# A transformer block in split fp32: the moving operand of every split matmul is read from its two halves in turn

## The chip, the cores and the metric

The kernel runs on one core of a Trainium2 chip. The metric is the device time of one execution in microseconds: the median of the runs of the kernel as it was is 2450.31 us. The engines are named as the profile names them: PE is TensorE (PEld its weight loads), DVE is VectorE, ACT is ScalarE, POOL is GpSimd, SP is the engine that issues most DMAs.

## The reference

One block over 2048 tokens of width 512, all in fp32. The first half is linear attention with 32 heads of 16 and a learned feature map; the second a mixture of 8 experts in which every token uses all 8 (K = E = 8), so nothing is sparse.

```python
h  = x + A(layernorm(x))
h2 = h + B(layernorm(h))

# A: x[S=2048, D=512], H=32 heads, Dh=16
q, k, v = split(x @ wqkv)
phi(q) = concat(softmax(q @ w_phi), softmax(-(q @ w_phi)))      # per head
o = phi_q (phi_k^T v) / (phi_q . sum(phi_k) + 1e-6)
A = o @ wo
# B: E=8 experts, F=1792
cw = softmax(x @ wg), normalized over all 8
B  = sum_e cw[:, e] * (gelu(x @ w1[e]) @ w2[e])
```

## The kernel before, in words

**Split products.** Each fp32 operand of the large products is split by `split` (lines 58 to 61) into a high part, which ScalarE rounds to the fp32r format, and a low part, the rest, which VectorE subtracts. A product of two split operands is three fp32r matmuls, `mm3` (lines 63 to 68): low times high, high times low, high times high, all added up in one PSUM tile. The first operand of `mm3` is stationary (128 columns of weights), the second is moving: 512 columns of a [128, 512] tile, read from the first to the last. Every matmul loads its own weights. All large products go through `mm3`: the projections (`project`), the experts' first layer (`product`), and the second layer (`product2`, `finish`).

**Stages.** The 2048 tokens are 16 tiles of 128 rows (`NT`), four tiles make a chunk of 512 (`TC`). In the attention stage `steps` walks over the tiles; a table `STAGES` gives each piece of work a lag, so that in one turn several tiles are in different pieces. There the tile of tokens, transposed, is stationary, and a projection weight [128, 512] is moving, so the 512 output columns are the 512 features. `fold` (line 119) multiplies the key and query weights by the feature maps beforehand: it transposes a weight on TensorE, and multiplies it by a block-diagonal [128, 128] matrix `bd`, which GpSimd builds at the start from `w_phi` with selects (lines 920 to 927). `wsplit` (line 101) splits the value and output weights as they are. `q_out` adds the attention's result to x and stores the tile of h in DRAM (`hbuf`); each tile of h is later read once, by `load_h` or in `finish`.

**Experts.** `q_ntrans` transposes the normalized h, so that 512 tokens of a chunk are the columns of a moving operand. The experts' products are arranged in blocks of 2 x 2 with seven products in place of eight (names `m1` to `m7`); their block sums are made on VectorE and split again. In the first layer (`quad`, `product`, into the PSUM tiles `ps`) the expert weights are stationary and 512 tokens move; ScalarE takes the gelu of the result, and VectorE multiplies it by the token's gate, which lies in the token's column of `CW` (loaded from `cwT`, one row of 512 gates per expert and chunk, made by `gate_rows`). In the second layer (`down`, `product2`, into `pacc`) that hidden block is the moving operand. Results are added up in DRAM by DMA (`macc`), and at the end `result` and `finish` load them, transpose them back to token rows, add h and store the output, 128 rows at a time.

**What sets the order.** The order on each engine is the order in which the code issues, with the lags of `STAGES` and the generators `moe`, `quad`, `fetch` and `result` interleaved. SP's queue issues loads of x, weights and h and stores of h and the output; POOL's queue issues the additions to `macc`. Tiles of SBUF come from two pools, `s4` (43 buffers) and `s2` (14), PSUM from `ps` and `pacc`, four banks each.

Of the kernel before, what the change touches and what calls it, by code (L numbers as in the profile page):

```python
# [8 lines left out]
F32 = mybir.dt.float32  # L9
F32R = mybir.dt.float32r  # L10
AF = mybir.ActivationFunctionType
ALU = mybir.AluOpType
AX = mybir.AxisListType

P = 128
# [6 lines left out]
def block_kernel(ctx: ExitStack, tc: tile.TileContext, x, wqkv, w_phi, wo, wg, w1, w2, out):  # L22
# [35 lines left out]
    def split(hi, lo, src, eng=nc.vector):  # L58

        nc.scalar.activation(hi, src, AF.Copy)  # L60
        return eng.tensor_tensor(lo, src, hi.bitcast(F32), op=ALU.subtract)  # L61

    def mm3(out_, a, b, first, last):

        (ah, al), (bh, bl) = a, b
        nc.tensor.matmul(out_, al, bh, start=first, stop=False, skip_group_check=True)  # L66
        nc.tensor.matmul(out_, ah, bl, start=False, stop=False, skip_group_check=True)  # L67
        nc.tensor.matmul(out_, ah, bh, start=False, stop=last, skip_group_check=True)  # L68
# [13 lines left out]


    st, low = {}, {}
    hbuf = [dram.tile([P, D], F32, name=f"h{t}") for t in range(NT)]
    cwT = dram.tile([E, S], F32, name="cwT")

    def load_x(lo, hi):
        for t in range(lo, hi):
            st["a", t] = s2()  # L90
            nc.sync.dma_start(st["a", t], x[t * P:(t + 1) * P, :])

    def load_w(w):

# [5 lines left out]

    def wsplit(src, eng=nc.vector):
        w = s4([P, 2, D], F32R)
        split(w[:, 0], w[:, 1], src, eng)
        return w[:, 0], w[:, 1]

    def split_all(raws, eng=nc.vector):
# [17 lines left out]
    def fold(raws, w, bd):  # L124

        wT = [s2() for _ in range(KD)]
        for b in range(KD):
            p = ps()
            for k in range(KD):
                nc.tensor.transpose(p[:, k * P:(k + 1) * P], raws[k // 2][:, k % 2, b * P:(b + 1) * P], ident)  # L130
            nc.scalar.activation(wT[b], p, AF.Copy)
            yield
        for k in range(KD):
            p = ps()
            for b in range(KD):
                nc.tensor.matmul(p[:, b * P:(b + 1) * P], wT[b][:, k * P:(k + 1) * P],  # L136
                                 bd[:, b].rearrange("p j f -> p (j f)"), start=True, stop=True)
            t = s4([P, 2, D], F32R)
            low["w"] = split(t[:, 0], t[:, 1], p)
            w.append((t[:, 0], t[:, 1]))  # L140
            yield

# [148 lines left out]

    def q_otrans(t):
        st["r", t] = s2()
        nc.sync.dma_start(st["r", t], x[t * P:(t + 1) * P, :])
        p = transposed(st.pop(("o", t)), ps_acc())
        o = st["O", t] = s4([P, 2, KD, P], F32R)
        split(o[:, 0], o[:, 1], p)

    def q_out(t):
        p = project(st.pop(("O", t)), wos, ps_acc())  # L300
        r = st["h", t] = st.pop(("r", t))
        nc.vector.tensor_tensor(r, p, r, op=ALU.add)
        nc.sync.dma_start(hbuf[t], r)
        norm_stats(r, t)


# [42 lines left out]
    def gate_rows(t, lag):  # L349

        c, j = divmod(t, TC)
        if j < TC - 1 or (c >= 2) != (lag > 29):
            return
        p = ps_acc()
        for j in range(TC):
            nc.tensor.transpose(p[:E, j * P:(j + 1) * P], cw[:, c * TC + j, :], ident)
        row = work.tile([E, 512], F32, name="row")
        nc.scalar.activation(row, p[:E], AF.Copy)
        nc.sync.dma_start(cwT[:, c * 512:(c + 1) * 512], row)

    X = {}
# [288 lines left out]

    def load_h(t, slot=s2):
        r = slot([P, D])
        nc.sync.dma_start(r, hbuf[t])
        return r

    def put_out(t, blocks, r):
# [36 lines left out]
    def finish(h, gs):  # L693

        old = {}

        def seeds(dst, src):
            for a, b in zip(dst, src):
                seed(a, b)

        def ready(m):
            for g in gs:
                if (g, m) not in G:
                    operand2(g, m)

        def add(g, m, p, first=False):
            for _ in product2(g, m, p, first):
                pass

        def run_(m, p):  # L710
            for g in gs:
                add(g, m, p)

        def block(i, c, p, r):
            for d in range(2):
                nc.vector.tensor_tensor(r[:, d], p[d], r[:, d], op=ALU.add)
            old[i, c] = r


        pa = [ps_acc(), ps_acc()]  # L720
        add(gs[0], "m1", pa, True)
        yield
        pd = [ps_acc(), ps_acc()]
        add(gs[0], "m5", pd, True)
        yield
        hs = [load_h(h * HALF + i, s4) for i in range(TC, HALF)]
        h0 = [s4([P, 2, D]) for _ in range(TC // 2)]
        for i, r in enumerate(h0):
            for j in range(2):
                nc.sync.dma_start(r[:, j, :], hbuf[h * HALF + 2 * i + j])  # L730
        pb, pc = [ps(), ps()], [ps(), ps()]
        for m in ("m5", "m6"):
            diffs(gs[1], m)
        operand2(gs[1], "m5")
        add(gs[1], "m1", pa)
        seeds(pb, pa)
        r11 = load_block(h, 0, 0)
        yield
        ready("m6")
        add(gs[1], "m5", pd)  # L740
        s5 = s4([P, 2, 512])
        for d in range(2):
            nc.scalar.activation(s5[:, d], pd[d], AF.Copy)
        for c in range(2):
            nc.gpsimd.dma_start(macc[h, BLOCK[c, 1]], s5, accum_op=ALU.add)
        yield
        ready("m2")
        run_("m6", pb)
        seeds(pc, pb)
        r22 = load_block(h, 1, 1)  # L750
        yield
        ready("m7")
        r12 = load_block(h, 0, 1)
        run_("m2", pa)
        block(0, 0, pa, r11)
        yield
        ready("m3")
        ready("m4")
        run_("m7", pc)
        block(1, 1, pc, r22)  # L760
        yield
        run_("m3", pb)
        r21 = load_block(h, 1, 0)
        block(0, 1, pb, r12)
        yield
        ops = [G.pop((g, "m4")) for g in gs]

        def last(d):
            sl = slice(d * P, (d + 1) * P)
            for (wh, wl), (xh, xl) in ops:  # L770
                for i in range(2):
                    mm3(pc[d], (wh[:, i, sl], wl[:, i, sl]), (xh[:, i], xl[:, i]), False, True)

        def sum_(d, i):

            sl = slice(i * 2 * P, (i + 1) * 2 * P)
            nc.vector.tensor_tensor(r21[:, d, sl], pc[d][:, sl], r21[:, d, sl], op=ALU.add)

        def back(d, p, i):

            src = (r11, r21)[d // 2][:, d % 2]
            for j in (2 * i, 2 * i + 1):
                nc.tensor.transpose(p[:, j * P:(j + 1) * P], src[:, j * P:(j + 1) * P], ident)
            o = h0[i][:, :, d * P:(d + 1) * P]
            nc.vector.tensor_tensor(o, p[:, i * 2 * P:(i + 1) * 2 * P].rearrange("p (j f) -> p j f", j=2), o, op=ALU.add)

        def store(lo, hi, i, eng=nc.sync):
            a = (h * HALF + 2 * i) * P
            eng.dma_start(out[a:a + 2 * P, lo * P:hi * P].rearrange("(j p) f -> p j f", p=P),
                              h0[i][:, :, lo * P:hi * P])  # L790

        def turn(d, p):
            if d >= 2:
                for i in range(2):
                    sum_(d - 2, i)
            for i in range(2):
                back(d, p[i], i)

        last(0)
        for d in range(2):  # L800
            turn(d, [ps_acc()] * 2)
        for t in range(TC, HALF):
            n = put_out(h * HALF + t, [r12, r22], hs[t - TC])
            put_store(h * HALF + t, hs[t - TC])
            if t == TC + 1:
                with tc.issue_after(n.ins):
                    turn(2, [ps_acc()] * 2)
                for i in range(2):
                    store(0, 3, i)
        with tc.issue_after(n.ins):  # L810
            last(1)
        turn(3, [ps_acc() for _ in range(2)])
        store(3, 4, 0, nc.scalar)
        store(3, 4, 1)
        yield
# [101 lines left out]
    norm_stats(st["a", 0], 0)  # L917


    bd = s2([P, H // HB, HB, Dh])  # L920
    for b in range(H // HB):
        nc.gpsimd.affine_select(out=bd[:, b], in_=phi_raw[:, b:b + 1, :].to_broadcast([P, HB, Dh]),
                                pattern=[[-Dh, HB], [0, Dh]], base=0, channel_multiplier=1,
                                compare_op=ALU.is_ge, fill=0.0)
        nc.gpsimd.affine_select(out=bd[:, b], in_=bd[:, b],
                                pattern=[[Dh, HB], [0, Dh]], base=Dh - 1, channel_multiplier=-1,
                                compare_op=ALU.is_ge, fill=0.0)

    x_norm(0)
# [37 lines left out]
```

## Time and profile before

| | us |
|---|---|
| median of 3 runs | 2450.31 (2450.18 to 2450.43) |
| span of the profiled execution | 2449.4 |
| PE busy | 2442.2 (100%) |
| PEld busy | 2037.8 (83%) |
| DVE busy | 2161.9 (88%) |
| ACT busy | 1759.9 (72%) |
| POOL busy | 500.4 (20%) |
| mean granted TensorE clock | 1.000 |

Busy time of PE counts overlapping matmuls once; the mean of a group of matmuls (389 to 391 ns for 512 columns) contains the part that overlaps its neighbours, and ends are modelled. The distance between starts says what one matmul costs in a row of them. The attention stage ends at about 340 us, the rest is the experts.

### The profile page before, as it was taken

To read this page: it belongs to the slowest core of one execution; us is meant where nothing else is said; L and a number is where in the kernel's file an instruction comes from. 1 tells how busy PE (TensorE), PEld (TensorE's weight loads), DVE (VectorE), ACT (ScalarE), POOL (GpSimd) and SP (SyncE) were. 2 spreads that over 40 slices of the span, in tenths; PEclk is the share of its full clock that TensorE was granted. 3 is DMA by queue.
4 is the path that set the end of the run, shared out by engine and by line. 5 is a ranking of instruction groups with operands and counts; after the bars stand their busy time and mean duration, and the time that the engine had idled before them with its cause. 6 is when DMAs were issued, how large, how long until landed. Compare 5 with 4: busy or idle time off the path is not lost.

```text
span 2449.4 us, 32135 instructions
## 1 busy us (share of the span) xinstructions
PE 2442.2 (100%) x11340; PEld 2037.8 (83%) x11340; DVE 2161.9 (88%) x3205; ACT 1759.9 (72%) x2891; POOL 500.4 (20%) x568
## 2 busy tenths in 40 slices
PE   9999999999999999999999999999999999999999
PEld 8888888888888888888888888888888888888887
DVE  7677999988989989889898998999889889898998
ACT  4343578777777777777777777777777777777774
POOL 4475101111111111111111331111111111111121
PEclk9999999999999999999999999999999999999999
DMA  3002347787777887877879898987877777877877
GB/s 113 26 14 70 109 173 164 146 168 158 147 158 151 164 165 140 169 151 151 166 143 206 180 203 159 227 174 153 161 157 150 159 163 148 168 143 163 160 154 183
DMA packets 174386, 370.80 MB, mean 151 GB/s; under 512 B 15216, under 2 KB 80240, under 8 KB 174224
## 3 DMA queue, kind: packets, MB, share of 16 engines
q0 software_dynamic: 62560, 206.60, 51.2%
q1 hardware_dynamic: 110336, 161.97, 20.6%
q8 instruction: 89, 1.46, 0.2%
q14 instruction: 73, 0.60, 0.1%
q10 hardware_dynamic: 1328, 0.18, 0.0%
HBM read 157.34 MB, written 218.69 MB: 154 GB/s over the span
## 4 chain that ended last, share of the span: by engine, by line
PE 98%; DVE 1%; ACT 0%; POOL 0%; issue 0%; ACTq 0%; POOLq 0%
PE pacc L66 16%; PE pacc L68 16%; PE pacc L67 16%; PE ps L66 15%; PE ps L68 15%; PE ps L67 15%; PE pacc L230 1%; PE ps L283 1%; PE pacc L161 1%; PE pacc L261 1%; PE pacc L332 0%; PE ps L136 0%; DVE s L61 0%; ACT s L60 0%; PE ps L113 0%; PE ps L161 0%
## 5 line engine op out<-in xcount | busy, mean ns | idle before, releaser
L61 DVE TENSOR_TENSOR s<-s,s 128x1024 fp32r<-128x1024 f32 (+1 forms) x806 | 762.8, 960 | 155.0 <-ACT s L60 146.2
L60 ACT ACTIVATE s<-s 128x512 fp32r<-128x512 f32 (+1 forms) x806 | 673.8, 842 | 11.6 <-DVE s L514 5.9
L66 PE MATMUL pacc<-s,s 128*128 128x512 f32 x1728 | 674.9, 391 | 0.8 <-ACT s L262 0.8
L67 PE MATMUL pacc<-s,s 128*128 128x512 f32 x1728 | 672.5, 389 | 0.3 <-DVE s L61 0.3
L68 PE MATMUL pacc<-s,s 128*128 128x512 f32 x1728 | 672.7, 389 | 0.0
L66 PE MATMUL ps<-s,s 128*128 128x512 f32 x1664 | 649.8, 391 | 0.2 <-ACT ps L569 0.2
L67 PE MATMUL ps<-s,s 128*128 128x512 f32 x1664 | 648.0, 389 | 0.0
L68 PE MATMUL ps<-s,s 128*128 128x512 f32 x1664 | 647.9, 389 | 0.0
L553 ACT ACTIVATE s<-pacc 128x512 f32<-128x512 f32 x756 | 447.0, 595 | 188.8 <-PE pacc L68 183.6
L564 ACT ACTIVATE ps<-ps 128x512 f32<-128x512 f32 x448 | 262.1, 586 | 175.3 <-DVE ps L616 106.0
L68 PEld LDWEIGHTS pacc<-s,s 128*128 128x128 f32 x1728 | 324.4, 188 | 67.9
L66 PEld LDWEIGHTS pacc<-s,s 128*128 128x128 f32 x1728 | 324.4, 188 | 67.5 <-ACT s L262 0.9
L67 PEld LDWEIGHTS pacc<-s,s 128*128 128x128 f32 x1728 | 324.4, 188 | 67.2 <-DVE s L61 0.8
L68 PEld LDWEIGHTS ps<-s,s 128*128 128x128 f32 x1664 | 312.3, 188 | 65.0
L66 PEld LDWEIGHTS ps<-s,s 128*128 128x128 f32 x1664 | 312.3, 188 | 64.5 <-ACT ps L569 0.5
L67 PEld LDWEIGHTS ps<-s,s 128*128 128x128 f32 x1664 | 312.5, 188 | 64.2 <-DVE s L61 0.3
L555 POOL DMA_DIRECT2D acc0m<-s x189 | 162.1, 858 | 856.9 <-ACT s L553 835.4
L565 DVE TENSOR_TENSOR s<-ps,s 128x512 f32<-128x512 f32 x448 | 302.9, 685 | 34.9 <-ACT ps L564 31.3
L555 POOL DMA_DIRECT2D acc1m<-s x175 | 149.5, 854 | 799.2 <-ACT s L553 782.6
L514 DVE TENSOR_TENSOR s<-s,s 128x1024 f32<-128x1024 f32 x224 | 272.9, 1219 | 0.1
L569 ACT ACTIVATE ps<-ps 128x512 f32<-128x512 f32 x226 | 132.0, 584 | 74.0 <-PE ps L68 73.8
L486 DVE TENSOR_TENSOR s<-s,s 128x1024 fp32r<-128x1024 f32 x111 | 135.0, 1216 | 0.0
(110 smaller groups left out, 1799.5 us busy)
## 6 DMA issues: line engine op xcount, KB each, us to landing
acc0m<-s POOLq DMA_DIRECT2D x196, 512.0 KB, 5.6
acc1m<-s POOLq DMA_DIRECT2D x184, 512.0 KB, 5.5
s<-in_B_w_dram SPq DMA_DIRECT2D x224, 256.0 KB, 5.7
s<-in_B_w_dram SPq DMA_DIRECT2D x111, 512.0 KB, 5.2
s<-in_A_x_dram SPq DMA_DIRECT2D x32, 256.0 KB, 2.8
s<-cwT SPq DMA_DIRECT2D x16, 512.0 KB, 5.0
h<-s SPq DMA_DIRECT2D x16, 256.0 KB, 2.0
s<-h SPq DMA_DIRECT2D x16, 256.0 KB, 7.0
```

Source lines behind the costliest of these rows:

```text
L60: nc.scalar.activation(hi, src, AF.Copy)
L61: return eng.tensor_tensor(lo, src, hi.bitcast(F32), op=ALU.subtract)
L66: nc.tensor.matmul(out_, al, bh, start=first, stop=False, skip_group_check=True)
L67: nc.tensor.matmul(out_, ah, bl, start=False, stop=False, skip_group_check=True)
L68: nc.tensor.matmul(out_, ah, bh, start=False, stop=last, skip_group_check=True)
L486: nc.vector.tensor_tensor(sl, s, sh.bitcast(F32), op=ALU.subtract)
L514: nc.vector.tensor_tensor(r, B[a], B[b], op=ALU.subtract)
L553: nc.scalar.activation(e[:, d], p[d], AF.Copy)
L555: return nc.gpsimd.dma_start(macc[h, m], e, accum_op=ALU.add)
L564: nc.scalar.activation(src, src, AF.Gelu_apprx_tanh)
L565: nc.vector.tensor_tensor(B[b][:, q % 2], src, CW[h, e][:, int(b[2]) - 1], op=ALU.mult)
L569: nc.scalar.activation(dst, src, AF.Copy)
```

## The change

`mm3` no longer reads the 512 columns of its moving operand from first to last. It reads columns 0, 256, 1, 257, 2, 258 and so on: one from the first half, one from the second. The output is written without steps, so output column 2a + b is made from moving column 256b + a. Three matmuls, their weights and their sizes are as before.

So that each product still comes out right, the data is laid out anew:

- **Projections.** Output columns are features. The moving weights now hold the even columns first and the odd columns second, so that reading the halves in turn gives the features in order. `wsplit` writes them so (its source is read with a step of two), and `fold` does so by a `bd` with even and odd features apart (eight selects 64 wide and four 128 wide, in place of four and four) and a stepped read of its PSUM tile.
- **Tokens.** Each of the experts' two layers moves the 512 tokens once, and turns their order once. A tile therefore holds every fourth row of its chunk of 512: tile r of chunk c has rows 512c + 4i + r. After two turns the tokens stand in natural order. The loads of x (`x_rows`) and the stores of h (`rows`) step over rows, 2 KB each as before; the loads of h take 128 rows in a row. h is now one DRAM tile per chunk.
- **Gates.** Between the two layers the tokens have been turned once, so `gate_rows` turns the gates' row once with a stepped read.

```diff
+    def halves(v):
+        return v.rearrange("p (b a) -> p a b", b=2)
+
     def mm3(out_, a, b, first, last):
-        (ah, al), (bh, bl) = a, b
+        (ah, al), (bh, bl) = a, (halves(v) for v in b)
+        out_ = out_.rearrange("p (a b) -> p a b", b=2)
         nc.tensor.matmul(out_, al, bh, start=first, stop=False, skip_group_check=True)
         nc.tensor.matmul(out_, ah, bl, start=False, stop=False, skip_group_check=True)
         nc.tensor.matmul(out_, ah, bh, start=False, stop=last, skip_group_check=True)
...
-    hbuf = [dram.tile([P, D], F32, name=f"h{t}") for t in range(NT)]
+    hbuf = [dram.tile([TC * P, D], F32, name=f"h{c}") for c in range(NT // TC)]
...
+    def rows(v, r):
+        return v.rearrange("(i r) d -> r i d", r=TC)[r]
+
+    def x_rows(t):
+        c, r = divmod(t, TC)
+        return rows(x[c * TC * P:(c + 1) * TC * P, :], r)
+
+    def h_rows(t):
+        c, j = divmod(t, TC)
+        return hbuf[c][j * P:(j + 1) * P, :]
...
     def wsplit(src, eng=nc.vector):
         w = s4([P, 2, D], F32R)
-        split(w[:, 0], w[:, 1], src, eng)
+        hi, lo = (w[:, i].rearrange("p (b a) -> p b a", b=2) for i in range(2))
+        split(hi, lo, src.rearrange("p (a b) -> p b a", b=2), eng)
         return w[:, 0], w[:, 1]
...
-                                 bd[:, b].rearrange("p j f -> p (j f)"), start=True, stop=True)
+                                 bd[:, b].rearrange("p l j f -> p (l j f)"), start=True, stop=True)
             t = s4([P, 2, D], F32R)
-            low["w"] = split(t[:, 0], t[:, 1], p)
+            hi, lo = (t[:, i].rearrange("p (l b w) -> p l b w", l=2, b=KD) for i in range(2))
+            low["w"] = split(hi, lo, p.rearrange("p (b l w) -> p l b w", l=2, b=KD))
...
-        nc.sync.dma_start(hbuf[t], r)
+        nc.sync.dma_start(rows(hbuf[t // TC], t % TC), r)
...
-        nc.scalar.activation(row, p[:E], AF.Copy)
+        nc.scalar.activation(row.rearrange("e (a b) -> e a b", b=2), halves(p[:E]), AF.Copy)
...
-    bd = s2([P, H // HB, HB, Dh])
+    bd = s2([P, H // HB, 2, HB, Dh // 2])
     for b in range(H // HB):
-        nc.gpsimd.affine_select(out=bd[:, b], in_=phi_raw[:, b:b + 1, :].to_broadcast([P, HB, Dh]),
-                                pattern=[[-Dh, HB], [0, Dh]], base=0, channel_multiplier=1,
-                                compare_op=ALU.is_ge, fill=0.0)
+        for l in range(2):
+            src = phi_raw[:, b:b + 1, :].rearrange("p o (f l) -> p o f l", l=2)[:, :, :, l]
+            nc.gpsimd.affine_select(out=bd[:, b, l], in_=src.to_broadcast([P, HB, Dh // 2]),
+                                    pattern=[[-Dh, HB], [0, Dh // 2]], base=0, channel_multiplier=1,
+                                    compare_op=ALU.is_ge, fill=0.0)
```

The order of the instructions on each engine is as before, but for two things. The first is on GpSimd at the start, where `bd` is built (`s_165` before, `s_153` after). Before:

```order
L152 TENSOR_TENSOR rs<-rs,mhalf 128x1
L80 AFFINE_SELECT hmask<-hmask 128x4
L922 AFFINE_SELECT s_165<-phi_raw 128x128 x2
L925 AFFINE_SELECT s_165<-s_165 128x128 x2
L922 AFFINE_SELECT s_165<-phi_raw 128x128 x2
L925 AFFINE_SELECT s_165<-s_165 128x128 x2
L152 TENSOR_TENSOR rs<-rs,mhalf 128x1 x2
```

After:

```order
L171 TENSOR_TENSOR rs<-rs,mhalf 128x1
L85 AFFINE_SELECT hmask<-hmask 128x4
L943 AFFINE_SELECT s_153<-phi_raw 128x64 x4
L946 AFFINE_SELECT s_153<-s_153 128x128 x2
L943 AFFINE_SELECT s_153<-phi_raw 128x64 x4
L946 AFFINE_SELECT s_153<-s_153 128x128 x2
L171 TENSOR_TENSOR rs<-rs,mhalf 128x1 x2
```

Four selects have become eight of half the width; the rest keeps its place. The second is on TensorE in the experts' part, where a first-layer product into `ps` is followed by a second-layer product into `pacc` (with what each instruction waits for; `PE_49` is TensorE's own count of finished work). Before:

```order
L66 MATMUL ps<-s_2861,s_9202 128x512 [waits Activation_49]
L67 MATMUL ps<-s_2862,s_9201 128x512
L68 MATMUL ps<-s_2861,s_9201 128x512
L66 MATMUL ps<-s_2861,s_9202 128x512
L67 MATMUL ps<-s_2862,s_9201 128x512
L68 MATMUL ps<-s_2861,s_9201 128x512
L66 MATMUL pacc<-s_9295,s_9292 128x512
L67 MATMUL pacc<-s_9296,s_9291 128x512 [waits DVE_49]
```

After:

```order
L71 MATMUL ps<-s_2853,s_9194 128x512 [waits Activation_49]
L72 MATMUL ps<-s_2854,s_9193 128x512
L73 MATMUL ps<-s_2853,s_9193 128x512
L71 MATMUL ps<-s_2853,s_9194 128x512
L72 MATMUL ps<-s_2854,s_9193 128x512
L73 MATMUL ps<-s_2853,s_9193 128x512
L71 MATMUL pacc<-s_9287,s_9284 128x512 [waits PE_49]
L72 MATMUL pacc<-s_9288,s_9283 128x512 [waits DVE_49]
```

The matmuls stand where they stood; the first into `pacc` now also waits for an earlier matmul of TensorE itself. The built program has 858 such waits, before it had 48.

More of the change, by code (lines that the diff above doesn't have):

```diff
@@ L90, in load_x @@
             st["a", t] = s2()
-            nc.sync.dma_start(st["a", t], x[t * P:(t + 1) * P, :])
+            nc.sync.dma_start(st["a", t], x_rows(t))
     def load_w(w):
@@ L293, in q_otrans @@
         st["r", t] = s2()
-        nc.sync.dma_start(st["r", t], x[t * P:(t + 1) * P, :])
+        nc.sync.dma_start(st["r", t], x_rows(t))
         p = transposed(st.pop(("o", t)), ps_acc())
@@ L652, in load_h @@
         r = slot([P, D])
-        nc.sync.dma_start(r, hbuf[t])
+        nc.sync.dma_start(r, h_rows(t))
         return r
@@ L729, in finish @@
             for j in range(2):
-                nc.sync.dma_start(r[:, j, :], hbuf[h * HALF + 2 * i + j])
+                nc.sync.dma_start(r[:, j, :], h_rows(h * HALF + 2 * i + j))
         pb, pc = [ps(), ps()], [ps(), ps()]
@@ L917, in block_kernel @@
     norm_stats(st["a", 0], 0)
-    bd = s2([P, H // HB, HB, Dh])
+    bd = s2([P, H // HB, 2, HB, Dh // 2])
     for b in range(H // HB):
-        nc.gpsimd.affine_select(out=bd[:, b], in_=phi_raw[:, b:b + 1, :].to_broadcast([P, HB, Dh]),
-                                pattern=[[-Dh, HB], [0, Dh]], base=0, channel_multiplier=1,
-                                compare_op=ALU.is_ge, fill=0.0)
+        for l in range(2):
[3 more added lines that the diff above has]
+                                    compare_op=ALU.is_ge, fill=0.0)
         nc.gpsimd.affine_select(out=bd[:, b], in_=bd[:, b],
-                                pattern=[[Dh, HB], [0, Dh]], base=Dh - 1, channel_multiplier=-1,
+                                pattern=[[0, 2], [Dh, HB], [0, Dh // 2]], base=Dh - 1, channel_multiplier=-1,
                                 compare_op=ALU.is_ge, fill=0.0)
```

## The prediction

> **What bounds the kernel now.** I read the page's totals first, then its chain of waits, then the groups of instructions, and last the windows and the timeline of TensorE alone.
>
> ```profile
> span 2449.4 us, 32135 instructions
> PE 2442.2 (100%) x11340; PEld 2037.8 (83%) x11340; DVE 2161.9 (88%) x3205; ACT 1759.9 (72%) x2891; POOL 500.4 (20%) x568
> PE 98%; DVE 1%; ACT 0%; POOL 0%; issue 0%; ACTq 0%; POOLq 0%
> L66 PE MATMUL pacc<-s,s 128*128 128x512 f32 x1728 | 674.9, 391 | 0.8 <-ACT s L262 0.8
> L67 PE MATMUL pacc<-s,s 128*128 128x512 f32 x1728 | 672.5, 389 | 0.3 <-DVE s L61 0.3
> L68 PE MATMUL pacc<-s,s 128*128 128x512 f32 x1728 | 672.7, 389 | 0.0
> L66 PE MATMUL ps<-s,s 128*128 128x512 f32 x1664 | 649.8, 391 | 0.2 <-ACT ps L569 0.2
> L67 PE MATMUL ps<-s,s 128*128 128x512 f32 x1664 | 648.0, 389 | 0.0
> L68 PE MATMUL ps<-s,s 128*128 128x512 f32 x1664 | 647.9, 389 | 0.0
> L66 PEld LDWEIGHTS ps<-s,s 128*128 128x128 f32 x1664 | 312.3, 188 | 64.5 <-ACT ps L569 0.5
> ```
>
> TensorE is never free: the chain that ended last is 98% its own, and the idle time ahead of its groups is under 1 us each. The three lines of a split product run 3 x (1728 + 1664) = 10,176 times with 512 columns each. Their 389 to 391 ns are not what one costs, since matmuls overlap; that is read from starts:
>
> ```profile
> 1200.09 0.39 PE L66 MATMUL ps<-s,s 128*128 128x512 f32 x1
> 1200.32 0.39 PE L67 MATMUL ps<-s,s 128*128 128x512 f32 x1
> ...
> 1211.65 0.39 PE L67 MATMUL ps<-s,s 128*128 128x512 f32 x1
> 1211.88 0.39 PE L68 MATMUL ps<-s,s 128*128 128x512 f32 x1
> ```
>
> From the first to the last of these lie 52 steps in 11.79 us: **227 ns per split matmul** (226.7). 10,176 of them take 2307 us, and the other 142 us of the span are transposes, narrow matmuls and the start. Is it something beside TensorE that sets the 227?
>
> ```profile
> 1300.00:1350.00 50.00, 50.00 (x222) 41.39 (x222) 42.29 (x56) 37.79 (x60) 7.69 (x9) 1.00 0.93 213
> 1350.00:1400.00 50.00, 50.00 (x222) 41.18 (x221) 48.33 (x70) 41.06 (x69) 14.30 (x17) 1.00 0.82 159
> 1700.00:1750.00 50.00, 50.00 (x223) 41.39 (x222) 44.90 (x65) 38.65 (x65) 8.06 (x10) 1.00 0.81 162
> 1850.00:1900.00 50.00, 50.00 (x222) 41.41 (x221) 45.17 (x64) 39.04 (x66) 7.71 (x9) 1.00 0.75 145
> ```
>
> (Columns: TensorE, weight loads, VectorE, ScalarE, GpSimd busy, each with its count; granted clock; DMA share; GB/s.) No: 222 or 223 matmuls start in each 50 us, whether VectorE is busy for 42 or 48 us of it and the DMA for 0.75 or 0.93, at a granted clock of 1.00. A weight load takes 188 ns, less than a step. So the 227 ns belong to the matmul itself, and the change alters just one thing in it: the order in which the moving operand's 512 elements are read.
>
> **The main term.** How much of the 227 ns could an order of reading take away or add? No row of this trace has a moving operand that is read with steps, so the cost is bounded by the nearest rows, the f32 transposes, which the change leaves alone:
>
> ```profile
> 201.00 0.60 PE L161 MATMUL pacc<-ident,s 128*128 128x128 f32 x4
> 201.44 1.90 PE L283 MATMUL ps<-s,s 128*128 128x68 f32 x16
> ...
> 203.17 1.04 PE L261 MATMUL pacc<-ident,s 128*128 128x128 f32 x8
> 203.97 0.47 PE L66 MATMUL pacc<-s,s 128*128 128x512 f32 x1
> 204.28 0.39 PE L67 MATMUL pacc<-s,s 128*128 128x512 f32 x1
> ```
>
> Four of them take 0.44 us, 110 ns for 128 columns, or 0.86 ns a column. Eight take 0.80 us, 100 ns each, but the split matmul behind them then takes 310 ns, 83 more than its 227; with those it is 110 again. A split column takes 227/512 = 0.44 ns, a little over half of 0.86. If the split format streams at just twice the f32 rate, 512 columns need 220 ns by the 110 and 200 by the 100. An f32 instruction's fixed share is counted twice in that 220, so the true figure is some nanoseconds below. I take **216 ns** as the rate of a read that never stalls (an estimate), which makes 10.7 ns of the 227 a stall. Solving for a fixed part F and equal streaming gives F = 2 x 110 - 227 = -7 ns: by these rows the excess lies in the stream, that is in the read, and not in a fixed cost of each instruction. The inference is weak where the transposes' own weight loads set the 110, because then the column rate is higher and some of the 227 may be fixed after all.
>
> The bounds of the unknown: the step can't go below the weight load's 188 ns (-39 ns, -394 us, where VectorE's 2161.9 us would bind first), and a read that delivers half as many columns per ns is what the f32 rows look like, 4 x 110 = 440 ns (+213 ns). Why I take a gain: the contiguous read stalls by the same amount in every window, so it is a pattern of the address stream; two streams 1 KB apart give each place that is read twice the time before its next piece is wanted. 10,176 x 10.7 ns = **-109 us**.
>
> The Trainium skill ("TensorE: Matmul & The Clock Gate", on the wait of 56 instead of 53.3 ns) gives 215.7 ns for back-to-back matmuls of 512 columns at full clock; this trace's 227 does not reach it, and by that figure the term would be 11.0 x 10,176 = 112 us.
>
> **The other terms.**
> VectorE: its work stays, in less time. Outside the busiest window it is 44 to 47 us per 50, and the same matmuls now take 47.6 us; the window at 1350 holds 48.33 us, so there and nearby TensorE waits a little. Bounds: 0 (buffers carry it) and 20 us (a slip of 0.5 us in each of some 40 windows). I take +8.
>
> Waits in TensorE's queue: the built program has 858 waits of TensorE on its own earlier matmuls, against 48 before. In the program the matmul named stands at least 26 places earlier (mostly 43), 26 x 0.216 = 5.6 us, so none should hold. They bring 327 more wait-only instructions.
>
> ```profile
> L136 PEldq EVENT_SEMAPHORE  x4: 51/51/51, 9.0 to 10.3; - x4
> ```
>
> At 51 ns that is 0 if the queue runs ahead, 17 us if not. Ahead of each step the loads leave 227 - 188 = 39 ns free, and the waits are spread over 2 ms: I take +1.
>
> Block-diagonal feature weights: GpSimd makes eight 64-wide selects in place of four 128-wide ones.
>
> ```profile
> 7.64 0.63 POOL L925 TENSOR_SCALAR_AFFINE_SELECT s<-s 128x128 f32<-128x128 f32 x2
> 8.23 2.07 ACT L131 ACTIVATE s<-ps 128x512 f32<-128x512 f32 x4
> 9.38 3.75 PE L136 MATMUL ps<-s,s 128*128 128x128 f32 x32
> 10.03 0.55 POOL L152 TENSOR_TENSOR rs<-rs,mhalf 128x1 f32<-128x1 f32 x1 [1.76 <-DVE rs L151]
> L922 POOL TENSOR_SCALAR_AFFINE_SELECT s<-phi_raw 128x128 f32<-128x128 f32 x4 | 1.4, 382 | 0.0
> ```
>
> Four more at 0 (half the width, half the time) to 0.38 us each push the last block from 8.27 to at most 9.8 us. The matmuls that use the blocks begin at 9.38 with the first, and the last must await ScalarE's transposed weights at 10.30. Queued behind on GpSimd is the power of tile 1 at 10.03. Hidden: 0, at most 1.5 us without that cover.
>
> Even columns first: sixteen splits on ScalarE and VectorE now step through their source. The nearest rows are two ScalarE copies, one that writes 16 elements of every 17 and one that writes all:
>
> ```profile
> L214 ACT ACTIVATE s<-pacc 128x512 f32<-128x512 f32 x16 | 9.5, 596 | 21.4 <-PE pacc L68 21.4
> L210 ACT ACTIVATE s<-pacc 128x512 f32<-128x512 f32 x16 | 9.5, 593 | 10.7 <-PE pacc L68 10.7
> s<-in_A_x_dram SPq DMA_DIRECT2D x32, 256.0 KB, 2.8
> h<-s SPq DMA_DIRECT2D x16, 256.0 KB, 2.0
> ```
>
> 596 against 593 ns: 0 for them. Doubled, the eight ahead of the first products would cost 8 x 0.6 = 5 us. The one strided gate row copy per 512 tokens has a whole later stage to land in.
>
> DMAs: tiles of x and h still move 128 rows of 2 KB, in the same order on SP's queue. Only the first x tile stands on the path (2.8 us); 0, at most +3 us if rows 8 KB apart took twice as long.
>
> **The sum.** 2449.4 - 109 + 8 + 1 = 2349.4 us span. The runs' median is 2450.31, 0.9 above the profiled span, so **2350 us**.
>
> **Rivals.**
> *The order of reading does nothing.* Then the 227 ns are fixed or set elsewhere, and only the small terms remain: 2450.3 + 1 to 2 = 2452 us. For it: the step is the same in every window, which a fixed cost would be too. Against: F came out negative above.
>
> *Alternation halves the read.* Two neighbours lie 4 bytes apart now and 1 KB apart afterwards. If the read port brings neighbours together, each pair needs two fetches from the first split matmul on, and a column takes the f32 rows' 0.86 ns: 440 ns per split matmul, 2449.4 + 10,176 x 0.213 = about 4620 us. It decides as soon as the spacing is above 228 ns. For it: a split column is read at nearly twice the rate of an f32 one, so something delivers it at a rate that two places may not sustain. Against: ScalarE's stepped copy costs nothing, though at 1.2 ns an element.
> The Trainium skill ("Advanced Engine Details and Errata", section on memory cachelines) speaks for this rival: SBUF has 16-byte lines, full speed needs two hits on a line, and a different line for each access is penalized. By that rule every element of the new order is such a crossing; no run here shows it yet for TensorE.
>
> *The gain is there but partial.* Half of the stall goes (221.4 ns): 2449.4 - 54 = 2395 us. It belongs to the forecast's own range.
>
> **How the numbers follow.** Faster 0.64 (the forecast with its partial form), nothing 0.16, halved read 0.20. The likeliest case's own range: from 214 ns with no VectorE wait (-129 us, 2320) to half the stall (2396). The range that should hold 8 in 10 reaches over the rival that does nothing: 2318 to 2460; what it leaves out is the halved read. A measurement of this kernel tells about 0.2%, 4.9 us, from no change, so the second case counts as same.
>
> **What would show it.** Right: starts of split matmuls 214 to 218 ns apart in the timeline, 229 to 234 of them in each 50 us window in place of 222, the f32 transposes still at 110, VectorE's share near 92% over the whole span, TensorE still the chain's owner. Wrong: 227 again (a fixed part), or 400 and more with VectorE and ScalarE half idle (lines). If spacing falls but the span doesn't follow, the chain will name VectorE's low halves (the second line of a split) ahead of matmuls.

## The result, and the profile after

The changed kernel takes 2349.66 us (median of 4 runs, 2348.30 to 2351.36), against 2450.37 us before: a ratio of 0.9587, 95% interval 0.9573 to 0.9600. The forecast was 2350.

The page of the changed kernel, the lines that answer to those of before (`mm3` is now lines 71 to 73):

```profile
span 2346.6 us, 32412 instructions
PE 2332.8 (99%) x11340; PEld 2049.4 (87%) x11340; DVE 2147.7 (92%) x3205; ACT 1739.6 (74%) x2891; POOL 501.0 (21%) x572
PE 86%; issue 3%; DMA 3%; DVE 2%; POOL 1%; ACT 1%; POOLq 0%; DVEq 0%; ACTq 0%; SPq 0%
L71 PE MATMUL pacc<-s,s 128*128 128x512 f32 x1728 | 657.2, 381 | 2.5 <-ACT s L281 0.8
L73 PE MATMUL pacc<-s,s 128*128 128x512 f32 x1728 | 654.9, 379 | 0.0
L73 PEld LDWEIGHTS ps<-s,s 128*128 128x128 f32 x1664 | 314.5, 189 | 44.4
s<-in_A_x_dram SPq DMA_DIRECT2D x32, 256.0 KB, 3.5
h<-s SPq DMA_DIRECT2D x16, 256.0 KB, 3.0
```

Each split matmul is 10 ns shorter, its weight load is as it was, and TensorE's busy time fell by 2442.2 - 2332.8 = 109.4 us. Its idle time, span less busy, grew from 7.2 to 13.8 us. Starts in the timeline, as before:

```profile
1200.19 0.38 PE L71 MATMUL pacc<-s,s 128*128 128x512 f32 x1
1200.41 0.38 PE L72 MATMUL pacc<-s,s 128*128 128x512 f32 x1
...
1211.63 0.38 PE L73 MATMUL ps<-s,s 128*128 128x512 f32 x1
1211.85 0.38 PE L71 MATMUL ps<-s,s 128*128 128x512 f32 x1
```

54 steps in 11.66 us are 215.9 ns each, against 226.7. In the windows TensorE still has no gap in nearly all of the experts' part, with 233 or 234 matmuls in 50 us; the main exceptions lie at 1250 to 1350 and 1500 to 1600 (columns as in the windows of the prediction):

```profile
1300.00:1350.00 50.00, 49.31 (x227) 42.26 (x226) 49.01 (x70) 41.42 (x70) 17.34 (x21) 1.00 0.85 172
1550.00:1600.00 50.00, 48.09 (x222) 41.84 (x223) 47.98 (x70) 40.77 (x70) 8.53 (x10) 1.00 0.82 157
1700.00:1750.00 50.00, 50.00 (x234) 43.77 (x233) 47.42 (x68) 39.95 (x67) 8.52 (x10) 1.00 0.78 150
```

### The profile page after: what moved, and what is told of

Read it like the earlier page. It is cut to its first block, busy times and chain, and to the rows that moved or that the text cites. A ratio compares the mean times of both kernels' runs of the same rounds, so it can differ in the third digit from the quotient of the medians.

```text
span 2346.6 us, 32412 instructions
## 1 busy us (share of the span) xinstructions
PE 2332.8 (99%) x11340; PEld 2049.4 (87%) x11340; DVE 2147.7 (92%) x3205; ACT 1739.6 (74%) x2891; POOL 501.0 (21%) x572
## 3 DMA queue, kind: packets, MB, share of 16 engines
q0 software_dynamic: 62560, 206.60, 53.3%
## 4 chain that ended last, share of the span: by engine, by line
PE 86%; issue 3%; DMA 3%; DVE 2%; POOL 1%; ACT 1%; POOLq 0%; DVEq 0%; ACTq 0%; SPq 0%
PE ps L71 14%; PE ps L72 14%; PE ps L73 14%; PE pacc L71 14%; PE pacc L73 14%; PE pacc L72 14%; DMA acc1m<-acc1m 1%; PE ps L302 1%; DMA out_dram<-s 1%; DVE s L61 1%; PE pacc L180 1%; PE pacc L280 1%; POOL acc1m L574 1%; PE pacc L351 1%; DMA acc1m<-s 0%
## 5 line engine op out<-in xcount | busy, mean ns | idle before, releaser
L71 PE MATMUL pacc<-s,s 128*128 128x512 f32 x1728 | 657.2, 381 | 2.5 <-ACT s L281 0.8
L72 PE MATMUL pacc<-s,s 128*128 128x512 f32 x1728 | 655.4, 379 | 0.4 <-DVE s L61 0.4
L73 PE MATMUL pacc<-s,s 128*128 128x512 f32 x1728 | 654.9, 379 | 0.0
L71 PE MATMUL ps<-s,s 128*128 128x512 f32 x1664 | 633.5, 381 | 3.3 <-DVE ps L635 1.9
L72 PE MATMUL ps<-s,s 128*128 128x512 f32 x1664 | 631.2, 379 | 0.6 <-DVE s L61 0.6
L73 PE MATMUL ps<-s,s 128*128 128x512 f32 x1664 | 630.8, 379 | 0.0
L572 ACT ACTIVATE s<-pacc 128x512 f32<-128x512 f32 x756 | 441.2, 593 | 139.1 <-PE pacc L73 135.1
L71 PEld LDWEIGHTS pacc<-s,s 128*128 128x128 f32 x1728 | 326.5, 189 | 49.3 <-issue 1.0
L72 PEld LDWEIGHTS pacc<-s,s 128*128 128x128 f32 x1728 | 326.7, 189 | 47.2 <-DVE s L61 1.8
L73 PEld LDWEIGHTS pacc<-s,s 128*128 128x128 f32 x1728 | 326.6, 189 | 46.2
L71 PEld LDWEIGHTS ps<-s,s 128*128 128x128 f32 x1664 | 314.4, 189 | 50.2 <-DVE ps L635 2.9
L72 PEld LDWEIGHTS ps<-s,s 128*128 128x128 f32 x1664 | 314.6, 189 | 44.7 <-DVE s L61 1.3
L73 PEld LDWEIGHTS ps<-s,s 128*128 128x128 f32 x1664 | 314.5, 189 | 44.4
```

What stands on the lines that cost most here:

```text
L572: nc.scalar.activation(e[:, d], p[d], AF.Copy)
```

## Experiments

### Undo the read alone, do the read alone

In the changed kernel the read goes back to first-to-last; in the kernel before, the read alone changes.

```diff
 # read undone, in the changed kernel
-        (ah, al), (bh, bl) = a, (halves(v) for v in b)
-        out_ = out_.rearrange("p (a b) -> p a b", b=2)
+        (ah, al), (bh, bl) = a, b
 # read alone, in the kernel before
-        (ah, al), (bh, bl) = a, b
+        (ah, al), (bh, bl) = a, (v.rearrange("p (b a) -> p a b", b=2) for v in b)
+        out_ = out_.rearrange("p (a b) -> p a b", b=2)
```

> The changed kernel with its whole new layout, but each split product reads its moving operand from first to last again (the output's columns therefore come out in another order than the reference's). Theory (the stall is in the contiguous read): split matmuls 227 ns apart again and the time of before, 2450 us within 3. Rival (the new layout or the new places of the tiles make the gain): 216 ns and 2350 us. Half and half, for instance 2400, would mean that both carry a part.

> The kernel before with nothing changed but the order in which mm3 reads its moving operand (columns come out in another order than the reference's). Theory: 216 ns between split matmuls and 2349 us within 4, so the new layout costs nothing. Rival that the layout makes the gain: 227 ns and 2450 us. If the layout costs something (stepped splits, strided rows), this kernel is faster than the changed one by that much, at most 5 us.

Measured: undone 2450.98 us, ratio to the kernel before 1.0005 (0.9995 to 1.0015). Alone 2349.61 us (2343.15 to 2351.34), ratio 0.9578 (0.9560 to 0.9596). TensorE's timeline of the first, then of the second:

```profile
1200.17 0.39 PE L71 MATMUL ps<-s,s 128*128 128x512 f32 x1
...
1203.57 0.39 PE L72 MATMUL ps<-s,s 128*128 128x512 f32 x1
```

```profile
1200.04 0.38 PE L69 MATMUL ps<-s,s 128*128 128x512 f32 x1
...
1203.93 0.38 PE L69 MATMUL pacc<-s,s 128*128 128x512 f32 x1
```

15 steps in 3.40 us are 226.7 ns; 18 steps in 3.89 us are 216.1 ns. The order of reading is the whole gain, and the new layout, with its stepped splits and rows, costs nothing that these medians can tell. That the layout makes the gain is ruled out.

### One matmul of three

In the changed kernel only the third matmul of a split product reads in halves, the first two first to last.

```diff
-        (ah, al), (bh, bl) = a, (halves(v) for v in b)
-        out_ = out_.rearrange("p (a b) -> p a b", b=2)
+        (ah, al), (bh, bl) = a, b
+        bt, turned = halves(bh), out_.rearrange("p (a b) -> p a b", b=2)
...
-        nc.tensor.matmul(out_, ah, bh, start=False, stop=last, skip_group_check=True)
+        nc.tensor.matmul(turned, ah, bt, start=False, stop=last, skip_group_check=True)
```

> The changed kernel with the halves read in turn in only one of the three matmuls of a split product, high times high (again with columns in another order). Theory (each matmul's own read stalls): the steps that belong to the two contiguous matmuls stay 227 ns, the third becomes 216, mean 223, time 2449 - 10,176/3 x 10.9 ns = 2412 us within 5. Rival (a step depends on what the neighbour reads too, for instance through a prefetch across instructions): all three steps change alike, or the total is off 2412 by more than 10 us.

Measured: 2428.39 us, 16 above the 2412 of the theory, so the rival was right that a step depends on its neighbours. The starts in one split product and the next:

```profile
1200.33 0.38 PE L73 MATMUL ps<-s,s 128*128 128x512 f32 x1
1200.54 0.39 PE L71 MATMUL ps<-s,s 128*128 128x512 f32 x1
1200.77 0.39 PE L72 MATMUL ps<-s,s 128*128 128x512 f32 x1
1201.00 0.38 PE L73 MATMUL ps<-s,s 128*128 128x512 f32 x1
```

Over the whole trace, without the few steps that hold other work or a wait (over 260 ns), the three steps are on average 215.1 ns from L73 (in halves) to L71, 231.5 from L71 to L72 and 227.3 from L72 to L73. A contiguous read right after one in halves costs 4 to 5 ns more than after another contiguous one. 673.9 ns a product in place of 669.2 (twice 226.7 and once 215.8), times 3392 products, is 16 us, which is the whole difference.

### The matmul by itself: which reads stall

A kernel of its own in place of the layer: groups of 64 matmuls with nothing beside them, each group with another read of the moving operand. The group in halves, for one:

```python
v = c.rearrange("p (b a) -> p a b", b=2)
for a, k in some():   # a: a PSUM bank, k: where the weights start
    nc.tensor.matmul(a[:128, :].rearrange("p (a b) -> p a b", b=2), w[:, k:k + 128], v, start=True, stop=True)
```

> No part of the block is computed: x is copied to the output, and TensorE runs groups of 64 matmuls into two PSUM tiles with the other engines idle, one source line per group, each with another read of its moving operand. Theory (the stall is in the stream of a contiguous fp32r read): contiguous 512 columns 227 ns also with idle neighbours; contiguous 384 and 320 columns 170 and 142 ns (in proportion); halves 216; 32 weight columns instead of 128 change nothing; bf16 216 with and without halves. Rival (a fixed 11 ns of each fp32r matmul, from its weights or its start): contiguous 384 and 320 columns 173 and 147 ns, and less with 32 weight columns. Which alternations help tells what the contiguous read stalls on: if any second stream will do, quarters, distances of 2 to 128 columns and a step of 2 all give 216; if the two places must be far apart, small distances stay at 227; if a step alone breaks the pattern, step 2 gives 216 without any alternation.

Here "halves" and "quarters" take one column from each half or quarter in turn, and a "distance" of 4 means pairs 4 columns apart inside blocks of 8 (0, 4, 1, 5 and so on). Timeline of TensorE; each row is one group of 64, so a group's step is the distance to the next row's start, divided by 64 (by 128 for f32, where each matmul is two instructions). Contiguous, halves, quarters, step 2, step 4; then distances 2, 4 and 8; then contiguous 384, halves 384, contiguous 320, contiguous from column 1, 32 weight columns; last bf16 contiguous, bf16 in halves, f32 contiguous:

```profile
32.56 14.67 PE L51 MATMUL acc<-m,w 128*128 128x512 f32 x64
47.07 13.97 PE L55 MATMUL acc<-m,w 128*128 128x512 f32 x64
60.88 18.28 PE L59 MATMUL acc<-m,w 128*128 128x512 f32 x64
79.00 29.04 PE L63 MATMUL acc<-m,w 128*128 128x512 f32 x64
107.86 29.70 PE L67 MATMUL acc<-m,w 128*128 128x512 f32 x64
...
217.62 14.71 PE L87 MATMUL acc<-m,w 128*128 128x512 f32 x64
232.18 13.98 PE L91 MATMUL acc<-m,w 128*128 128x512 f32 x64
245.99 13.98 PE L95 MATMUL acc<-m,w 128*128 128x512 f32 x64
...
315.06 11.27 PE L115 MATMUL acc<-m,w 128*128 128x384 f32 x64
326.17 10.56 PE L119 MATMUL acc<-m,w 128*128 128x384 f32 x64
336.57 9.55 PE L123 MATMUL acc<-m,w 128*128 128x320 f32 x64
345.96 15.29 PE L127 MATMUL acc<-m,w 128*128 128x512 f32 x64
361.09 14.98 PE L131 MATMUL acc<-m,w 128*32 128x512 f32 x64
...
389.73 13.99 PE L139 MATMUL acc<-mb,wb 128*128 128x512 bf16 x64
403.55 31.16 PE L143 MATMUL acc<-mb,wb 128*128 128x512 bf16 x64
434.55 55.09 PE L147 MATMUL acc<-src 128*128 128x512 f32 x128
```

| read of the moving operand | ns per matmul |
|---|---|
| fp32r, 512 columns, contiguous | 226.7 |
| halves (0, 256, 1, 257) | 215.8 |
| quarters (0, 128, 256, 384, 1) | 283 |
| runs of two from each half (0, 1, 256, 257) | 328.6 |
| step 2 (all even, then all odd) | 451 |
| pairs 2 columns apart | 227.5 |
| pairs 4 or 8 columns apart | 215.8 |
| contiguous, from column 1 | 236.4 |
| 384 columns: contiguous, halves | 173.6, 162.5 |
| 320 columns, contiguous | 146.7 |
| 32 weight columns: contiguous, halves | 231.6, 215.9 |
| bf16, 512 columns: contiguous, halves | 216, 484 |

Two things follow. The 227 ns have nothing to do with other engines, which idle here. And the excess doesn't grow with the columns: from 320 to 384 to 512 columns a contiguous read takes 26.9 and 53.1 ns more, 0.42 ns a column or 2.4 columns per ns, as halves do (53.3 ns from 384 to 512). At 384 and at 512 columns it is the same 11 ns above halves. My theory that the stream stalls fell here; the first rival's "fixed cost" was right, but it is a fixed cost that the order of reading takes away.

Three more expectations missed. In bf16 two streams were expected to change nothing, and a matmul took 484 ns in place of 216. With 32 weight columns the rival expected less, and a contiguous matmul took more (231.6). And none of the three rules about alternation holds: two streams help from 4 columns apart on, but not at 2, and four streams and plain steps cost more than the contiguous read.

### What the fixed 11 ns hang on

> No part of the block is computed: x is copied to the output, and TensorE runs groups of 64 (or 63) matmuls, one source line per group. After the first such run the stall is a fixed amount of each contiguous fp32r matmul (13.4 ns over 512, 384 or 320 columns at 2.4 columns per ns, 2.5 for halves). Theory A (it is the start of a contiguous read, whose first lines arrive late): contiguous 480, 448 and 256 columns still have 13.4 ns (213.4, 200.1, 120.1), halves 256 has 2.5 (109.2, or what the weight load allows), the start's place in its line matters (from 1: 236), weights and PSUM banks don't matter. Theory B (the weight load that runs beside it takes slots of the read): 64 and 96 weight columns take other times than 128 in proportion, and weights read with a step change it. Theory C (PSUM): one bank in place of two changes it. Mixed sequences, if each matmul has its own cost: by turns 221.2, two contiguous and one in halves 223.1, one and two 219.4; what is above that is the cost of a change of pattern. Distances that put neighbours in different 16-byte lines (5, 6, 8) 202.5 ns for 480 columns, distance 3, where one pair in three shares a line, between that and 213.4 if lines decide.

Contiguous, halves, by turns, two and one, one and two, 64 and 96 weight columns; contiguous from 16, halves from 1, distance 4 from 2; contiguous 480, 448 and 256, halves 256, distances 3 and 5 with 480 columns. Groups with 63 matmuls are divided by 63; the steps of rows that aren't shown come from the same view:

```profile
32.28 14.67 PE L55 MATMUL acc<-m,w 128*128 128x512 f32 x64
46.79 13.98 PE L60 MATMUL acc<-m,w 128*128 128x512 f32 x64
60.60 14.46 PE L65 MATMUL acc<-m,w 128*128 128x512 f32 x64
74.89 14.30 PE L70 MATMUL acc<-m,w 128*128 128x512 f32 x63
89.03 14.06 PE L75 MATMUL acc<-m,w 128*128 128x512 f32 x63
102.93 14.90 PE L80 MATMUL acc<-m,w 128*64 128x512 f32 x64
117.66 14.89 PE L85 MATMUL acc<-m,w 128*96 128x512 f32 x64
...
222.48 14.81 PE L120 MATMUL acc<-m,w 128*128 128x512 f32 x64
237.13 14.03 PE L125 MATMUL acc<-m,w 128*128 128x512 f32 x64
250.99 14.68 PE L130 MATMUL acc<-m,w 128*128 128x512 f32 x64
265.51 14.03 PE L135 MATMUL acc<-m,w 128*128 128x480 f32 x64
279.38 13.13 PE L140 MATMUL acc<-m,w 128*128 128x448 f32 x64
292.35 7.84 PE L145 MATMUL acc<-m,w 128*128 128x256 f32 x64
300.02 7.31 PE L150 MATMUL acc<-m,w 128*128 128x256 f32 x64
307.17 16.38 PE L155 MATMUL acc<-m,w 128*128 128x480 f32 x64
323.38 14.68 PE L160 MATMUL acc<-m,w 128*128 128x480 f32 x64
```

- Theory A, the start of the read, holds only roughly in the columns. Contiguous 256 take 119.9 ns (120.1 expected), 106.7 of it at 2.4 columns per ns, so 13.2 over. Contiguous 480 and 448 take 216.8 and 202.7 (213.4 and 200.1 expected) and have 16 to 17 over, so the excess isn't the same for every width, though it doesn't grow in proportion. Halves 256 take 111.7, 5 over in place of the 2.5 at 512. The start's place counts too, though A gave a figure only for column 1, 236: from column 1, 2, 4, 8 and 16 a contiguous read takes 236.8, 233.4, 231.6, 233.4 and 228.8; halves from column 1 take 216.6.
- Theory C, PSUM, fell: one bank instead of two keeps the step at 226.7.
- Theory B, the weight load, isn't clean. 32, 64 and 96 weight columns take 231.6, 230.2 and 230.1, none of them in proportion and all above the 226.7 of 128, while the load itself gets shorter (109, 134 and 161 ns against 188); the same weights each time take 227.1. With weights read in steps of 4 both contiguous and halves take longer (234.9 and 237.6); there a load lasts 309 and 334 ns and may itself be the bound, so that part tells nothing.
- A change of pattern costs: by turns 223.4 (221.2 expected), two contiguous and one in halves 224.4 (223.1), one and two 220.6 (219.4), as in the kernel with one of three.
- Sixteen-byte lines alone don't decide. With 480 columns pairs 6 and 8 columns apart take the expected 202.5, but 5 columns 226.9 and 3 columns 253.3, more than a contiguous read; and pairs 4 columns apart that start at column 2 lose their gain (226.8), while halves that start at column 1 keep it.

So the excess is a cost of each contiguous fp32r read that doesn't grow with its columns, 13 to 17 ns above 2.4 columns per ns when it starts at column 0 and up to 24 when it starts elsewhere. Two streams from column 0 that lie 4, 6, 8 or more columns apart, always an even number here, bring it down to 2.5 ns at 384 columns and more. That it sits at the boundary of two matmuls is likely, since it doesn't grow with the columns, but not shown. What is late there (the first lines of a read, or how they meet the next weight load) stays open: no run here separates the read from its weight load, since every fp32r matmul loads its own.

### Two streams near each other, inside the kernel

```diff
 # in the kernel before
+        (ah, al), (bh, bl) = a, (v.rearrange("p (o b a) -> p o a b", b=2, a=4) for v in b)
+        out_ = out_.rearrange("p (o a b) -> p o a b", b=2, a=4)
```

> The kernel before with mm3 reading column pairs 4 columns (16 bytes) apart, inside blocks of 8 columns (0, 4, 1, 5, ...), and nothing else changed (columns come out in another order than the reference's). Theory (neighbours in different 16-byte lines are enough): 216 ns between split matmuls and 2350 us within 4, as for halves. Rival (inside the kernel, with ScalarE, VectorE and the DMAs writing the memory, two streams must be far apart): more than 2360 us.

Measured: 2349.29 us (2346.78 to 2350.62), ratio 0.9589 (0.9573 to 0.9605). The theory holds inside the kernel too: 16 bytes are far enough, so the columns need be turned only inside blocks of 8.

### Where the rest of the gain went, and a faster version

The chain of waits of the changed kernel between 1540 and 1560 us, and TensorE's timeline there:

```profile
1542.59 8.04 DMA out_dram<-s
1550.74 1.15 ACT s L60 x2
```

```profile
1549.06 0.38 PE L73 MATMUL ps<-s,s 128*128 128x512 f32 x1
1551.30 0.48 PE L71 MATMUL ps<-s,s 128*128 128x512 f32 x1 [1.85 <-DVE ps L635]
```

A split on ScalarE needs a small tile (`s2`) that still holds output rows on their way to DRAM, 8 us long; VectorE works late behind it, and TensorE idles for 1.85 us, and for another 0.6 at 1557. Two kernels take that away in two ways: the rows of h go into large tiles, or there are 16 small and 42 large tiles in place of 14 and 43.

```diff
-        rows = [load_h(h * HALF)]
+        rows = [load_h(h * HALF, s4)]
...
-                rows.append(load_h(t + 1))
+                rows.append(load_h(t + 1, s4))
```

```diff
-SLOTS = 43
-HALF_SLOTS = 14
+SLOTS = 42
+HALF_SLOTS = 16
```

> The changed kernel with the rows of h that the first half's result is built on held in the large tiles instead of the small ones, which the splits of the second layer's weights also use. In the changed kernel TensorE waits 3.2 us near 1551 us behind a split on ScalarE that awaits an output store. Theory (the store holds the small tile): that wait goes, 2346 to 2347 us. Rival (another tile is short next): 2349 to 2352 us.

> The changed kernel with 16 small and 42 large tiles in place of 14 and 43 (the same memory). Theory (small tiles are short): the waits near 1300 and 1551 us shrink, 2345 to 2348 us. Rival (the large tiles are short as well): above 2350 us, with TensorE waiting for splits into large tiles.

Measured: 2344.84 us (2344.19 to 2347.52) and 2345.98 us (2345.32 to 2349.82). A window of the first shows TensorE without a gap there:

```profile
1550.00:1600.00 50.00, 50.00 (x234) 43.80 (x233) 48.31 (x69) 40.37 (x69) 8.51 (x10) 1.00 0.81 153
```

Both were compared with the kernel before only, so the first was timed once more beside the changed kernel.

> The changed kernel itself, on the same chip as the next one: 2349 us within 2, with the waits of TensorE near 1551 us.

> The changed kernel with the rows of h in large tiles, timed a second time beside the changed kernel. Theory (the wait near 1551 us is gone and nothing comes in its place): 2 to 4 us less than the changed kernel on the same chip. Rival (the first time was chance): the same within 1 us.

Measured on one chip: changed kernel 2350.45 us (2348.30 to 2353.05, 5 runs), with rows in large tiles 2345.00 us (2344.61 to 2347.12, 4 runs); the two don't overlap. Their ratios to the kernel before are 0.9593 (0.9580 to 0.9606) and 0.9569 (0.9556 to 0.9582). The version with large tiles has the lowest median of all, 105 us below the kernel before; its range overlaps that of the version with 16 small tiles. Its gain of some 5 us is more than the 2.5 us that TensorE idles between 1500 and 1600 in the trace of the changed kernel (the expectation had 3.2). Much of the rest goes with the granted clock. The changed kernel's two executions at 2348.30 have a mean clock of 1.000 and its other seven 0.998 or 0.999; all eight of the version with large tiles have 1.000. Among those at 1.000 the gain is 2348.3 - 2345.0 = 3.3 us, and 0.001 of 2350 us is some 2.4 us (an estimate from these two numbers), about what the median execution loses. What lowers the clock wasn't traced. Nor does the wait come in every execution: the profiled one of the read alone, with the same tiles, has none between 1500 and 1600, and that of the near streams has 3.0 us.

## Why the prediction was right

- **What bounds the kernel**: right. TensorE's own step set the time, and nothing beside it set the step; the matmul by itself shows the same 226.7 ns.
- **The main term**: its size was right, 10.7 ns foretold and 10.9 measured, 109 us foretold and 109.4 of TensorE's busy time measured. The reason given for it was wrong. The step that failed is "the excess lies in the stream, that is in the read, and not in a fixed cost of each instruction", from F = -7. Solving for F gave the f32 rows and the contiguous split read the same fixed part. The runs show two. From 320 to 512 columns a contiguous split matmul streams at 0.417 ns a column, which leaves a fixed 13.4 ns of its 226.7, and 2.5 of the 215.8 in halves. An f32 instruction takes 429 ns for 512 columns ((489.48 - 434.55) / 128, the next group starting at 489.48); with the prediction's 110 for 128 that is 0.83 ns a column and a fixed 3.6. Twice 3.6 less 13.4 is -6, so an F below zero comes out of a fixed cost of the contiguous read as well.
- **Luck in the main term**: the 216 ns were no luck, since the f32 rows do stream at half the rate, and their 220 less a fixed share of 3.6 is 216.4. That this order of reading would reach them was in part luck. The reason, two streams that leave each place more time, would have spoken as well for four streams (283) and for pairs 2 columns apart (227.5), neither of which gains; and the 1 KB between the streams was not the point, since 16 bytes do.
- **The lower bound of 188 ns**, the length of a weight load, was no bound: 256 columns in halves take 111.7 ns a step while each load lasts 192, so loads overlap. Only the small term for the waits in the queue leaned on it.
- **The rival of a fixed cost** was right that the excess doesn't grow with the columns and wrong in the consequence: it is not immune to the order of reading.
- **The rival of a halved read** didn't come for halves, but it exists next door: step 2 takes 451 ns, near the 440 foretold, and bf16 in halves 484. The Trainium skill's rule of 16-byte lines ("Advanced Engine Details and Errata", section on memory cachelines) by itself would have condemned the halves and the pairs 4 columns apart as well, and both run at 215.8, so the runs decide against it for fp32r in two streams. The Trainium skill's 215.7 ns ("TensorE: Matmul & The Clock Gate", section "Wait — 56ns, not 53.3ns?") is met by the contiguous bf16 matmuls (216) and by fp32r only in two streams.
- **VectorE, +8**: idle time grew by 6.6 us, so the size was about right, but by luck: only a small part is where it was put. The window at 1300, with 49.01 us of VectorE work, has 0.7 us of it; the largest piece, 2.5 us in 1500 to 1600, is the small tile behind an output store, and 2.1 us of the growth lie in the first 340 us, mostly the attention stage.
- **Waits in the queue, +1**: nothing to be seen; TensorE has no gap in nearly all of the windows, over which these waits are spread.
- **Selects, splits, DMAs at 0**: the median of the kernel with the read alone is that of the changed one (2349.61 against 2349.66). The profiled executions, all at a clock of 1.000, hint at a small cost: less TensorE's idle time between 1500 and 1600, the two kernels in the old layout take 2341.4 and 2342.1 us (read alone, near streams), the changed one and the one with rows in large tiles 2344.1 and 2343.7. That is some 2 us for the layout, from one execution each. Loads of x did land later, 3.5 us in place of 2.8, and stores of h 3.0 in place of 2.0.

## What to carry to other kernels

When an engine is busy all the time, look at the distance between starts, not at the mean duration: a constant step that no other engine changes points to the instruction itself, and its operands' access patterns are a thing to vary. For contiguous fp32r matmuls of 512 columns here the step has 11 ns too many, and reading two streams 4, 8 or more columns apart, from column 0, takes them away. Four streams, plain steps, two streams 2 or 3 columns apart and bf16 don't gain here, and most of them cost far more. Time such a pattern alone before laying data out for it: one small kernel with a group per pattern told more than the whole kernel could.

## What was not expected of the hardware

A read in two alternating streams is faster than a contiguous one (215.8 against 226.7 ns), while four streams (283), runs of two from each half (328.6), or bf16 in the same two streams (484 against 216) are far slower. The excess of a contiguous read doesn't grow with its columns but depends on where it starts (228.8 to 236.8 ns from columns 1 to 16, 226.7 from column 0), and a contiguous read costs 4 to 5 ns more behind one in two streams. Fewer weight columns made contiguous matmuls slower, not faster (231.6 ns with 32).
